# Omega and the first row-wise load on two DMA queues, the activation table first, and more tiles for batch 0's rows

## The chip, the core and the metric

The kernel runs on one core of a Trainium2 chip. A core has a matrix engine (TensorE, PE; its weight loads are shown as PEld), a vector engine (VectorE, DVE), a scalar engine (ScalarE, ACT), a general engine (GpSimd, POOL) and a synchronisation engine (SyncE, SP) that here issues the DMA transfers. Each engine works through its own instruction list in order and waits on semaphores. The metric is the device time of one execution in microseconds (us), lower is better.

## The reference

Three stages follow one another. The first is linear attention with exponential random features, for 4 batches of 8 heads, 576 rows and 64 columns; the other two are feed-forward layers over the 2304 resulting rows of 512.

```python
def phi(x):                                   # x = q*scale or k*scale
    proj = np.einsum('bhsd,md->bhsm', x, omega)          # 128 features
    sq = np.sum(x * x, axis=-1, keepdims=True) / 2.0
    h = proj - sq
    h = h - np.max(h, axis=-1, keepdims=True)
    return np.exp(h) / np.sqrt(m)
q_p, k_p = phi(q_s), phi(k_s)
kv = np.einsum('bhsm,bhsd->bhmd', k_p, v);  z = np.sum(k_p, axis=2)
out = einsum(q_p, kv) / (einsum(q_p, z) + 1e-06)
x = out.transpose(0, 2, 1, 3).reshape(B * S, H * D)      # 2304 x 512
h = np.maximum(x @ w_in, 0.0);  x = h * h @ w_out        # 512 -> 2048 -> 512
xn = x / rms * rms_g;  out = (silu(xn @ w_gate) * (xn @ w_val)) @ w_out2   # 512 -> 1536 -> 512
```

## The kernel before, in words

The kernel is written as a list of steps (`plan.add`): each has an engine, an estimated duration, a priority, a function that emits its instructions, and the buffers that it reads and writes. `Plan.run` (line 113) simulates these steps on the engines with the estimated durations, takes the ready step with the lowest priority number on each free engine, gives out tiles from numbered classes (`slots`, line 301) as they come free, and so writes the order in which the instructions stand on every engine. What the simulation decides is fixed in the program; on the chip each engine follows that order and waits by semaphores where an input isn't there. A step may have alternatives on another engine (`alts`); the planner takes the one that it expects to end first. Three constants matter here: matrix steps count double before `COLD`; from 0.6 to 45.0 us of planned time (`FILL`) the planner puts pairs of dummy matmuls with a matrix of ones (line 480) where TensorE has nothing to do; a DMA (line 383) occupies the SyncE queue for its bytes at 311 KB per us and lands 2.0 us later.

Attention goes batch by batch (`attention(b)`, line 519) and in it by four pairs of heads. A pair loads transposed k and q (tile classes `lt` and `tt`), row-wise k and q (class `ld`, three tiles) and v. The row-wise loads are only for the squared norms: one step squares the tile in place (line 496; on GpSimd, ScalarE or VectorE, lines 498 to 500), a VectorE step sums it (line 531). The feature matmuls (line 577) take the transposed loads and `oms`, which is omega turned and scaled. Maxima are taken on VectorE (line 584), the two corrections join them (line 589), and ScalarE takes the exponentials (line 596). Products with v, transposes and a division follow, and the pair's result is split in two parts of reduced width for the dense stage (lines 392 and 401). What is left of 576 rows after 512 is loaded for all heads at once (`rest_t`, `rest_r`, `rest_v`).

The first feed-forward layer (`moe1`) has for each batch 16 blocks of hidden units: line 804 is its first product, line 834 its second. While batch 0 is in this layer its weights are loaded, decoded on VectorE and ScalarE (lines 430 to 444) and split; attention of batch 1 is interleaved with it. Class `f` has four tiles, which hold the outputs of `relu` in that layer (line 818). The second feed-forward layer comes last (lines 1046 and 1107).

At the start, omega is loaded twice by two transfers on SyncE's queue (line 386, called from line 486), into the lower and the upper 64 partitions of `om2`; ScalarE scales it into `oms` (line 489). That instruction is the first one on ScalarE, and the load of the activation table stands in front of it.

Of the kernel before, what the change touches and what calls it, by code (L numbers as in the profile page):

```python
# [9 lines left out]
F32 = mybir.dt.float32  # L10
# [4 lines left out]
AF = mybir.ActivationFunctionType  # L15
ALU = mybir.AluOpType
# [26 lines left out]
class Plan:  # L43
# [8 lines left out]

    COLD = 6.9
    FILL = (0.6, 45.0, 0.21)
    SPARE = {"DVE": 1.0, "ACT": 0.2, "POOL": 0.2}
    SPARE_TO = 200.0
# [54 lines left out]
    def run(self):  # L113
# [9 lines left out]
        slot = {}  # L123
        engs = sorted({n.eng for n in self.nodes})
        ready = {e: [] for e in engs}
        busy = {e: 0.0 for e in engs}
        held_by = {"DVE": 0.0}
        events = []
        seq = 0
# [1 line left out]
        def push(t, kind, n):  # L131
            nonlocal seq
            seq += 1
            heapq.heappush(events, (t, seq, kind, n))
# [17 lines left out]
        avail = {}  # L152
        for n in self.nodes:
            if n.ndeps == 0:
                push(0.0, 0, n)
        spare_bank = None
        if self.filler:
            c = self.filler[0].classes[0]
# [4 lines left out]
        while done < len(self.nodes):  # L163
# [4 lines left out]
            while events and events[0][0] <= now + 1e-9:  # L168
                _, _, kind, n = heapq.heappop(events)
# [3 lines left out]
                elif kind == 1:  # L173
# [7 lines left out]
                    for o in n.outs:  # L181
                        o.ndeps -= 1
                        t = now + (self.SAME.get(n.eng, 0.0) if o.eng == n.eng and not n.tail else self.LAT)
# [6 lines left out]
            for e in engs:  # L190
# [5 lines left out]
                while ready[e]:  # L196
                    item = heapq.heappop(ready[e])
                    n = item[3]
# [25 lines left out]
                if pick is not None:  # L224
# [3 lines left out]
                    if isinstance(pick.dur, Shared):  # L228
                        start = max(now, busy["POOL"])
                        held_by["DVE"] = start + pick.dur  # L230
                    busy[e] = start + pick.dur * (2.0 if e == "PE" and now < self.COLD else 1.0)
                    push(busy[e] + pick.tail, 1, pick)
# [5 lines left out]
        for n in order:  # L238
            for b in n.acq:
                c, s = slot[b]  # L240
                t = self.alloc[c](s)
# [6 lines left out]
def kernel(  # L248
# [23 lines left out]
    nc = tc.nc  # L272
    PSUM = bass.MemoryType.PSUM
    B, SR, H, _ = rest_v.shape
    _, HP, P, _, R, D = q_r.shape
# [10 lines left out]
    SCALE = float(D) ** -0.25  # L286
# [4 lines left out]
    const = ctx.enter_context(tc.tile_pool(name="const", bufs=1))  # L291
# [16 lines left out]
    plan = Plan(slots)  # L308
# [38 lines left out]
    ones = const.tile([P, P], F32R, name="ones")  # L347
    om2 = const.tile([P, M], F32, name="om2")
    oms = const.tile([P, M], F32, name="oms")
    g_sb = const.tile([P, KC], F32, name="g_sb")  # L350
    eps_sb = const.tile([P, 1], F32, name="eps_sb")
    v_t = [att.tile([P, 2, R, D + 1], F32, name=f"v{i}") for i in range(2)]
    vr_t = att.tile([P, H * (D + 1) + 8], F32, name="vr")[:, :H * (D + 1)].rearrange("p (h n) -> p h n", h=H)
    kv_t = [att.tile([P, 2, 80], F32, name=f"kv{i}")[:, :, :D + 1] for i in range(2)]
# [4 lines left out]
    b_oms = Buf(ap=oms)  # L359
# [7 lines left out]
    def f32(t):  # L367
        return t.bitcast(F32)
# [11 lines left out]
    def pe(n, cnt, passes=1):  # L380
        return cnt * passes * max(0.109, 0.0133 + n / 2400.0)

    def dma(prio, outap, inap, nbytes, r=(), w=(), after=()):
        return plan.add(
            "SP", nbytes / 311e3, prio,
            lambda: nc.sync.dma_start(out=outap(), in_=inap()), r, w, after, tail=2.0,
        )

# [21 lines left out]
    def load_unit(prio, dst, src, r=(), after=()):  # L410

        wap, c = src
        wide = wap.dtype != F32
        words = 2 if wide else 1
        a = wap[c].bitcast(U32) if wide else wap[c]
        o = (lambda: dst.ap.rearrange("p n t -> p (n t)")) if wide else (lambda: dst.ap)
        dma(prio, o, lambda: a, 262144 * words, r=list(r), w=[dst], after=after)
# [43 lines left out]
    T0 = -40.0  # L461
# [10 lines left out]
    b_late, b_eps = Buf(ap=ones), Buf(ap=eps_sb)  # L472
# [8 lines left out]
                             rhs=ones.rearrange("p (o n) -> p o n", o=1).to_broadcast([P, 2, P]), start=True, stop=True)  # L481

    plan.filler = Buf(["acc"]), filler
    b_om = Buf(ap=om2)
    for h in range(2):
        dma(T0, lambda h=h: om2[h * D:(h + 1) * D, :], lambda: omega_t, 32768, w=[(b_om, h)])
    dma(T0 + 30, lambda: g_sb, lambda: rms_g.rearrange("(k p) -> p k", p=P), 2048, w=[b_g])

    plan.add("ACT", 0.4, T0, lambda: nc.scalar.activation(out=oms, in_=om2, func=AF.Copy, scale=SCALE), [b_om], [b_oms])

    def copy(prio, out, src, n, rd, wr):

# [26 lines left out]
    def attention(b):  # L519
# [7 lines left out]
        def row_norms(prio, x, ss):  # L527
            square(prio, x, lambda: x.ap, 512)
            plan.add(
                "DVE", dve(512), prio,  # L530
                lambda: nc.vector.tensor_reduce(out=ss.ap[:, :8], in_=x.ap, op=ALU.add, axis=AX), [x], [ss],
            )

        def operand(ldp, src, cls):

            x = Buf(["lt", cls])
            dma(ldp, lambda: x.ap, src, 262144, w=[x])
            return x

        def rem_prep(pr0):  # L540
            rem_x[:] = [operand(lead, lambda: rest_t[b].rearrange("p h n -> p (h n)"), "tr")]
            xr = Buf(["ld"], view=lambda t: t.rearrange("p h r d -> p (h r) d"))
            dma(lead, lambda: xr.ap, lambda: rest_r[b], 262144, w=[xr])
            row_norms(pr0, xr, ssr)
            dma(lead, lambda: vr_t[P - SR:], lambda: rest_v[b], 133120, w=[b_vr])

        def pair(hp):
# [7 lines left out]
            ld = pb - 3.0  # L555
# [3 lines left out]
            def transposed(nm, p0):  # L559
                ss = stats[nm] = Buf(["sm"])  # L560
                src, src_t = (k_r, k_t) if nm == "k" else (q_r, q_t)
                xs = operand(ld, lambda: src_t[b, hp], "tt")
                x = Buf(["ld"], view=lambda t: t.rearrange("p h r d -> p (h r) d"))
                dma(ld + 0.05, lambda: x.ap, lambda: src[b, hp].rearrange("p h r d -> p (h r) d"), 262144, w=[x])
                row_norms(p0, x, ss)
                return xs

# [35 lines left out]
            u = step / 10.0  # L603
            pk, pq = Buf(["p"]), Buf(["p"])
            xk = transposed("k", pb)
            features(pb + u, pk, xk, ODD, stats["k"], list(last_q))
            if hp == 0:
                rem_prep(pb + u)
                rem_p[:] = [Buf(["pr"])]
                features(pb + 2 * u, rem_p[0], rem_x[0], ODD, ssr)  # L610
            pr = rem_p[0]
            xq = transposed("q", pb + 2 * u)
            last_q[:] = [features(pb + 4 * u, pq, xq, ODD, stats["q"])]

# [558 lines left out]


    attention(0)
    for b in range(B):
        if b + 1 < B:
            attention(b + 1)
        moe1(b)
# [104 lines left out]
```

## Time and profile before

| | us |
|---|---|
| median of three runs | 972.69 (971.24 to 972.92) |
| the profiled execution, its own time | 972.6 |
| its span, first to last instruction | 970.8 |
| TensorE busy in it | 955.1 |
| VectorE busy | 688.4 |
| ScalarE busy | 518.6 |
| GpSimd busy | 78.8 |

The profile is one execution. The times of rows are microseconds from the start of the span unless marked ns. A row of a timeline names start, length, engine, line, operation and tiles (out <- in); in brackets stands how long the engine had been idle before, and what ended that. SPq is the issue of a DMA on SyncE. PE's granted clock is shown as a share of 2.4 GHz. A table by stretch gives for each stretch its length, the busy time of PE, PEld, DVE, ACT and POOL with the number of instructions, the granted clock, the busy share of the DMA engines, and the GB/s that they moved.

### The profile page before, as it was taken

What the parts mean: (1) busy time and instruction counts of PE and PEld (TensorE: products, weight loads), DVE (VectorE), ACT (ScalarE), POOL (GpSimd) and SP (SyncE); (2) the same over time, 40 slices, a digit from 0 to 9 for tenths busy, and PEclk for the clock granted to TensorE, in tenths of its full rate; (3) what the DMA queues carried; (4) which work ended last, traced back from release to release, by engine and by line L of the source; (5) the groups of instructions that cost most, each with busy time, mean ns of one, the idle gap of its engine ahead of it and who ended that gap; (6) DMA issues with size and microseconds to landing.
All of it is one profiled execution on the core that took longest, in us unless ns stands there. A gap on an engine that the chain in (4) does not pass through costs nothing.

```text
span 970.8 us, 16150 instructions
## 1 busy us (share of the span) xinstructions
PE 955.1 (98%) x6036; PEld 793.0 (82%) x6036; DVE 688.4 (71%) x1241; ACT 518.6 (53%) x1078; POOL 78.8 (8%) x69
## 2 busy tenths in 40 slices
PE   8999999999999999999999999999999999999998
PEld 7877777787888788788889888888878888888886
DVE  5889988756747556645745889989897757577573
ACT  6987788656446446445645658554443452323220
POOL 1123312000101010000100110000000000000000
PEclk9999999999999999999999999999999999999999
DMA  7878788888678565598978444324233221222203
GB/s 248 271 255 285 245 283 310 284 305 293 223 238 284 185 222 176 181 309 280 317 254 316 127 142 124 105 88 133 87 107 131 77 76 33 77 61 59 70 29 108
DMA packets 74845, 179.45 MB, mean 185 GB/s; under 512 B 8848, under 2 KB 12048, under 8 KB 74768
## 3 DMA queue, kind: packets, MB, share of 16 engines
q1 hardware_dynamic: 74768, 178.43, 56.0%
q8 instruction: 47, 0.77, 0.3%
q14 instruction: 30, 0.25, 0.1%
HBM read 143.27 MB, written 35.13 MB: 184 GB/s over the span
## 4 chain that ended last, share of the span: by engine, by line
PE 82%; DVE 8%; DMA 4%; ACT 3%; issue 1%; POOL 1%; SPq 0%; POOLq 0%; DVEq 0%; ACTq 0%
PE h L804 17%; PE acc L834 17%; PE acc L1046 12%; PE t L1107 11%; PE h L1046 11%; PE t L1046 4%; PE t L577 3%; DMA st<-in_w_gate_dram 1%; DMA ld<-in_k_r_dram 1%; PE t L692 1%; PE t L635 1%; DVE cc L1066 1%; PE acc L480 1%; PE t L686 1%; PE h L1107 1%
## 5 line engine op out<-in xcount | busy, mean ns | idle before, releaser
L834 PE MATMUL acc<-g,wr 128*128 128x512 f32 (+1 forms) x660 | 151.5, 373 | 1.2 <-POOL g L392 1.2
L804 PE MATMUL h<-x,wr 128*128 128x512 f32 x528 | 134.6, 398 | 0.0
L834 PEld LDWEIGHTS acc<-g,wr 128*128 128x128 f32 x660 | 113.4, 189 | 22.2 <-POOL g L392 1.4
L401 ACT CAST wq<-wq 128x512 fp32r<-128x512 f32 x108 | 66.5, 619 | 103.2 <-DMA wq<-w2d4g 15.8
L1107 PE MATMUL t<-wq,ub 128*128 128x512 f32 x474 | 116.7, 391 | 1.4 <-DVE oa L1115 1.3
L804 PEld LDWEIGHTS h<-x,wr 128*128 128x128 f32 x528 | 97.6, 189 | 21.7
L1046 PE MATMUL acc<-x,wq 128*128 128x512 f32 x324 | 106.9, 389 | 0.0
L1107 PEld LDWEIGHTS t<-wq,ub 128*128 128x128 f32 x474 | 88.4, 188 | 22.2 <-DVE oa L1115 2.9
L392 DVE TENSOR_TENSOR wq<-wq 128x512 fp32r<-128x512 f32 x108 | 79.7, 745 | 30.4 <-ACT wq L401 30.0
L818 ACT ACTIVATE f<-h 128x512 f32<-128x512 f32 (+1 forms) x80 | 44.9, 562 | 90.1 <-PE h L804 90.1
L1046 PE MATMUL h<-x,wq 128*128 128x512 f32 x252 | 85.3, 390 | 0.0
L392 DVE TENSOR_TENSOR g<-f,g 128x512 fp32r<-128x512 f32 (+1 forms) x61 | 39.6, 650 | 45.6 <-ACT f L499 34.5
L1046 PEld LDWEIGHTS acc<-x,wq 128*128 128x128 f32 x324 | 60.8, 188 | 12.8 <-DVE cc L1066 0.2
L1046 PE MATMUL acc<-xa,wq 128*128 128x512 f32 x192 | 69.8, 389 | 0.0
L834 PE MATMUL acc<-g,wu 128*128 128x512 f32 (+1 forms) x300 | 68.3, 373 | 0.0
L1066 DVE TENSOR_TENSOR cc<-acc,cc 128x512 f32<-128x512 f32 x84 | 57.8, 688 | 14.3 <-PE acc L1046 13.1
L1115 DVE TENSOR_TENSOR oa<-t,oa 128x512 f32<-128x512 f32 x75 | 50.9, 688 | 21.8 <-PE t L1107 21.3
L596 ACT ACTIVATE p<-t,sm 128x128 f32<-128x128 f32 x212 | 57.8, 382 | 14.2 <-DVE sm L589 12.2
L439 ACT ACTIVATE dw<-st 128x512 f32<-128x512 f32 x68 | 46.4, 692 | 29.2 <-DMA st<-in_w_out_dram 8.7
L804 PE MATMUL h<-x,wu 128*128 128x512 f32 x240 | 61.5, 399 | 0.0
L1046 PE MATMUL h<-xa,wq 128*128 128x512 f32 x168 | 60.5, 389 | 0.0
L834 PEld LDWEIGHTS acc<-g,wu 128*128 128x128 f32 x300 | 51.7, 189 | 9.6
(213 smaller groups left out, 1641.5 us busy)
## 6 DMA issues: line engine op xcount, KB each, us to landing
wr<-w1d SPq DMA_DIRECT2D x88, 512.0 KB, 4.6
st<-in_w_out_dram SPq DMA_DIRECT2D x28, 512.0 KB, 4.9
w1d<-wr SPq DMA_DIRECT2D x22, 512.0 KB, 4.3
st<-in_w_in_dram SPq DMA_DIRECT2D x16, 512.0 KB, 4.5
st<-in_w_gate_dram SPq DMA_DIRECT2D x12, 512.0 KB, 5.5
st<-in_w_val_dram SPq DMA_DIRECT2D x12, 512.0 KB, 5.2
st<-y SPq DMA_DIRECT2D x23, 256.0 KB, 4.2
v<-in_v_r_dram SPq DMA_DIRECT2D x16, 260.0 KB, 4.2
```

The costliest lines, as they stand in the source:

```text
L392: return lambda: en.tensor_tensor(out=lo(), in0=src(), in1=f32(hi()), op=ALU.subtract)
L401: first = plan.add("ACT", act(n), prio, lambda: nc.scalar.copy(out=hi(), in_=src()), rd, [whi], after, pre=[blo] if blo is not bhi else [])
L439: lambda: nc.scalar.activation(out=out(), in_=hf(), func=AF.Abs, scale=65536.0), [(st, 1)], [w])
L577: nc.tensor.matmul(fps[h].ap[:, i, :], lhsT=x.ap[ps, c], rhs=oms[ps, :], start=True, stop=True)
L596: nc.scalar.activation(out=pbuf.ap[:, j, :], in_=fp.ap[:, i, :], func=AF.Exp, bias=mx.ap[:, j:j + 1])
L804: nc.tensor.matmul(hb.ap[:, :n], lhsT=u.ap[:, wl, kk * P:(kk + 1) * P], rhs=xcols(j, xl, kk)(), start=(gi == 0 and ii == 0), stop=(gi == l ...
L818: lambda: nc.scalar.activation(out=rb.ap[:, :n], in_=hb.ap[:, :n], func=AF.Relu), [hb], [rb])
L834: nc.tensor.matmul(accs[e].ap[:, :n], lhsT=u.ap[:, w, es], rhs=x.ap[:, :n], start=(c == 0 and i == 0), stop=(c == C1 - 1 and i == 2))
L1046: nc.tensor.matmul(bank.ap[:, cols], lhsT=u.ap[:, wl, c0 + kk * P:c0 + (kk + 1) * P], rhs=x[kk][xl].ap[:, :cols.stop - cols.start], start= ...
L1066: lambda: nc.vector.tensor_tensor(out=out.ap, in0=bank.ap, in1=x.ap, op=ALU.add), [bank, x], [out])
L1107: nc.tensor.matmul(o.ap, lhsT=x[xl].ap[:, c0:c0 + P], rhs=us[f"o{i}"].ap[:, wl, :], start=i == n == 0, stop=i == 1 and n == 2)
L1115: lambda: nc.vector.tensor_tensor(out=oa.ap, in0=o.ap, in1=oa.ap, op=ALU.add), [o, oa], [oa])
```

## The change

Omega's second half is loaded by a DMA that ScalarE issues; so is the first row-wise k of batch 0, whose priority is raised to that of omega. An exponential of one column of ones is written to a new small tile (`warm`), so that it is ScalarE's first activation. Omega is scaled on VectorE. The row-wise loads of batch 0 (k, q and the rest) may take a tile of class `f` where no `ld` tile is free. In the planner, all engines begin at 0.75 us, matrix steps count double until 8.0 us, a DMA on SyncE occupies the queue for at least 0.45 us, and one on ScalarE occupies that engine for 0.6 us and lands 2.6 us later.

```diff
--- before.py
+++ after.py
@@ -52,7 +52,8 @@
 
 
 
-    COLD = 6.9
+    BEGIN = 0.75
+    COLD = 8.0
     FILL = (0.6, 45.0, 0.21)
     SPARE = {"DVE": 1.0, "ACT": 0.2, "POOL": 0.2}
     SPARE_TO = 200.0
@@ -123,7 +124,7 @@
         slot = {}
         engs = sorted({n.eng for n in self.nodes})
         ready = {e: [] for e in engs}
-        busy = {e: 0.0 for e in engs}
+        busy = {e: self.BEGIN for e in engs}
         held_by = {"DVE": 0.0}
         events = []
         seq = 0
@@ -152,7 +153,7 @@
         avail = {}
         for n in self.nodes:
             if n.ndeps == 0:
-                push(0.0, 0, n)
+                push(self.BEGIN, 0, n)
         spare_bank = None
         if self.filler:
             c = self.filler[0].classes[0]
@@ -349,6 +350,7 @@
     oms = const.tile([P, M], F32, name="oms")
     g_sb = const.tile([P, KC], F32, name="g_sb")
     eps_sb = const.tile([P, 1], F32, name="eps_sb")
+    warm = const.tile([P, 1], F32, name="warm")
     v_t = [att.tile([P, 2, R, D + 1], F32, name=f"v{i}") for i in range(2)]
     vr_t = att.tile([P, H * (D + 1) + 8], F32, name="vr")[:, :H * (D + 1)].rearrange("p (h n) -> p h n", h=H)
     kv_t = [att.tile([P, 2, 80], F32, name=f"kv{i}")[:, :, :D + 1] for i in range(2)]
@@ -380,9 +382,11 @@
     def pe(n, cnt, passes=1):
         return cnt * passes * max(0.109, 0.0133 + n / 2400.0)
 
-    def dma(prio, outap, inap, nbytes, r=(), w=(), after=()):
+    def dma(prio, outap, inap, nbytes, r=(), w=(), after=(), act_queue=False):
+        if act_queue:
+            return plan.add("ACT", 0.6, prio, lambda: nc.scalar.dma_start(out=outap(), in_=inap()), r, w, after, tail=2.6)
         return plan.add(
-            "SP", nbytes / 311e3, prio,
+            "SP", max(0.45, nbytes / 311e3), prio,
             lambda: nc.sync.dma_start(out=outap(), in_=inap()), r, w, after, tail=2.0,
         )
 
@@ -481,12 +485,15 @@
                              rhs=ones.rearrange("p (o n) -> p o n", o=1).to_broadcast([P, 2, P]), start=True, stop=True)
 
     plan.filler = Buf(["acc"]), filler
-    b_om = Buf(ap=om2)
-    for h in range(2):
-        dma(T0, lambda h=h: om2[h * D:(h + 1) * D, :], lambda: omega_t, 32768, w=[(b_om, h)])
+    b_om, b_warm = Buf(ap=om2), Buf(ap=warm)
+    dma(T0, lambda: om2[:D], lambda: omega_t, 32768, w=[(b_om, 0)])
+    dma(T0, lambda: om2[D:], lambda: omega_t, 32768, w=[(b_om, 1)], act_queue=True)
+    plan.add("ACT", 1.4, T0 + 6.0, lambda: nc.scalar.activation(out=warm, in_=f32(ones[:, :1]), func=AF.Exp), [b_late],
+             [b_warm], after=[plan.nodes[-1]])
     dma(T0 + 30, lambda: g_sb, lambda: rms_g.rearrange("(k p) -> p k", p=P), 2048, w=[b_g])
 
-    plan.add("ACT", 0.4, T0, lambda: nc.scalar.activation(out=oms, in_=om2, func=AF.Copy, scale=SCALE), [b_om], [b_oms])
+    plan.add("DVE", 0.2, T0, lambda: nc.vector.tensor_scalar(out=oms, in0=om2, scalar1=SCALE, scalar2=None, op0=ALU.mult),
+             [b_om], [b_oms])
 
     def copy(prio, out, src, n, rd, wr):
 
@@ -531,6 +538,9 @@
                 lambda: nc.vector.tensor_reduce(out=ss.ap[:, :8], in_=x.ap, op=ALU.add, axis=AX), [x], [ss],
             )
 
+        def by_rows(t):
+            return t.rearrange("p h r d -> p (h r) d") if len(t.shape) > 2 else t.rearrange("p (n d) -> p n d", d=D)
+
         def operand(ldp, src, cls):
 
             x = Buf(["lt", cls])
@@ -539,7 +549,7 @@
 
         def rem_prep(pr0):
             rem_x[:] = [operand(lead, lambda: rest_t[b].rearrange("p h n -> p (h n)"), "tr")]
-            xr = Buf(["ld"], view=lambda t: t.rearrange("p h r d -> p (h r) d"))
+            xr = Buf(["ld"] if b else ["ld", "f"], view=by_rows)
             dma(lead, lambda: xr.ap, lambda: rest_r[b], 262144, w=[xr])
             row_norms(pr0, xr, ssr)
             dma(lead, lambda: vr_t[P - SR:], lambda: rest_v[b], 133120, w=[b_vr])
@@ -560,8 +570,9 @@
                 ss = stats[nm] = Buf(["sm"])
                 src, src_t = (k_r, k_t) if nm == "k" else (q_r, q_t)
                 xs = operand(ld, lambda: src_t[b, hp], "tt")
-                x = Buf(["ld"], view=lambda t: t.rearrange("p h r d -> p (h r) d"))
-                dma(ld + 0.05, lambda: x.ap, lambda: src[b, hp].rearrange("p h r d -> p (h r) d"), 262144, w=[x])
+                x = Buf(["ld"] if b else ["ld", "f"], view=by_rows)
+                dma(T0 if b == hp == 0 and nm == "k" else ld + 0.05, lambda: x.ap,
+                    lambda: src[b, hp].rearrange("p h r d -> p (h r) d"), 262144, w=[x], act_queue=b == hp == 0 and nm == "k")
                 row_norms(p0, x, ss)
                 return xs
 
```

## Rows read from the trace of the kernel before

**Rows 1.** The page's busy times: engine, us, share of the span, instructions

```profile
PE 955.1 (98%) x6036; PEld 793.0 (82%) x6036; DVE 688.4 (71%) x1241; ACT 518.6 (53%) x1078; POOL 78.8 (8%) x69
```

**Rows 2.** Table by stretch: stretches of the prologue and after it

```profile
20.00:54.00 34.00, 32.82 (x504) 28.26 (x503) 30.73 (x85) 30.59 (x86) 5.12 (x4) 1.00 0.84 288
...
60.00:80.00 20.00, 19.78 (x142) 15.69 (x141) 18.22 (x30) 18.32 (x46) 8.77 (x7) 1.00 0.70 226
...
240.00:300.00 60.00, 60.00 (x450) 48.23 (x449) 37.03 (x81) 32.04 (x74) 3.59 (x5) 1.00 0.71 237
```

**Rows 3.** Timeline of the first 12 us, all engines

```profile
0.74 1.22 SPq L386 DMA_DIRECT2D om<-in_omega_t_dram  x2
...
0.83 0.17 DVE L464 MEMSET ones<- 128x128 f32 x1 [0.83 <-PEq L1272]
...
1.05 2.64 PEld L480 LDWEIGHTS acc<-ones 128*128 128x128 f32 x12 [1.05 <-DVE ones L464]
...
2.00 0.58 SPq L386 DMA_DIRECT2D lt<-in_k_t_dram  x1
...
3.10 0.43 SPq L386 DMA_DIRECT2D ld<-in_k_r_dram  x1
...
3.61 1.28 ACT L489 ACT_TABLE_LOAD   x1 [3.61 <-DMA om<-in_omega_t_dram]
...
5.27 1.78 PEld L577 LDWEIGHTS t<-oms,lt 64*128 64x128 f32 x16 [1.58 <-ACT oms L489]
...
7.24 1.27 ACT L499 ACTIVATE ld<-ld 128x512 f32<-128x512 f32 x2 [2.02 <-DMA ld<-in_k_r_dram]
...
7.90 0.69 DVE L531 TENSOR_REDUCE sm<-ld 128x8 f32<-128x512 f32 x1 [6.90 <-ACT ld L499]
...
10.56 0.63 ACT L499 ACTIVATE ld<-ld 128x512 f32<-128x512 f32 x1 [2.05 <-DMA ld<-in_rest_r_dram]
...
11.09 2.15 ACT L596 ACTIVATE p<-t,sm 128x128 f32<-128x128 f32 x8
```

**Rows 4.** Chain that ended last, first 20 us: start, length, what

```profile
4.53 5.25 DMA tr<-in_rest_t_dram
...
14.67 2.59 PE acc L480 x20
```

**Rows 5.** Chain that ended last, 40 to 62 us

```profile
44.90 4.77 DMA ld<-in_k_r_dram
...
54.47 5.91 PE h L804 x18
```

**Rows 6.** Waits from 40 to 54 us: total, times, longest

```profile
ACT ld L499 <- DMA ld<-in_k_r_dram: 1.2, 1, 1.2
```

**Rows 7.** Table by stretch, single microseconds before and in the dense stage

```profile
52.00:53.00 1.00, 0.48 (x2) 0.29 (x2) 0.95 (x3) 0.99 (x3) 0.37 (x1) 1.00 0.74 299
...
55.00:56.00 1.00, 1.00 (x4) 0.81 (x3) 1.00 (x3) 0.67 (x2) 0.00 (x0) 0.50 0.69 234
```

**Rows 8.** Chain that ended last, near 100 us

```profile
100.18 3.00 PE h L804 x12
```

**Rows 9.** Table by stretch, the first transfers

```profile
3.10:4.10 1.00, 0.88 (x5) 0.59 (x3) 0.00 (x0) 0.49 (x1) 0.00 (x0) 1.00 0.82 196
4.10:8.10 4.00, 2.83 (x26) 2.83 (x28) 0.20 (x1) 1.96 (x4) 0.00 (x0) 1.00 1.02 353
```

**Rows 10.** VectorE to 54 us, by line: busy us, mean ns, idle before

```profile
L444 DVE SCALAR_TENSOR_TENSOR dw<-dw,st 128x512 uint32<-128x512 uint32 x4 | 2.7, 685 | 0.0
...
L435 DVE SCALAR_TENSOR_TENSOR st<-st 128x512 uint32<-128x512 uint32 x3 | 2.0, 683 | 0.0
...
L392 DVE TENSOR_TENSOR wr<-dw,wr 128x512 fp32r<-128x512 f32 x2 | 1.3, 671 | 0.0
```

**Rows 11.** Waits of SyncE's queue, 0 to 20 and 20 to 46 us

```profile
SPq L386 <- DVE sm L531: 1.1, 2, 0.8
...
SPq L386 <- DVE sm L531: 2.1, 2, 1.5
```

## The prediction

> **What bounds the kernel now.** I read the page's busy shares first. TensorE is busy for 98% of the span [rows 1], so time can be won in two ways only: less matmul work, or matmul work that starts earlier. The diff touches no matmul, so the second is the question. The table by stretch says where TensorE is full with useful work: from 54 us on it is busy nearly all the time (60.00 of 60.00 us in the third row) [rows 2]. Between 20 and 54 us it looks full as well, but there it runs the dummy matmuls of line 480 in its pauses, and VectorE (30.73 of 34.00 us) and ScalarE (30.59) are the engines that carry the attention of batch 0 [rows 2]. So the first 54 us are a prologue: what ends it earlier moves the whole rest of the kernel forward, and what only fills it does nothing.
>
> The start of the prologue, in order of time [rows 3]: SyncE needs from 0.74 to 1.96 us for the two omega loads, and only then issues the transposed k (2.00) and, fourth in line, the row-wise k (3.10). ScalarE waits for omega until 3.61, loads its table for 1.28 us, and scales omega; the first feature matmul starts at 5.27. The dummy matmuls stand at 0.22 us each (2.64 us for 12), nearly twice what they take later (20 in 2.59 us, [rows 4]). ScalarE's first square waits 2.02 us for the row-wise k, until 7.24, and VectorE does nothing useful before 7.90. ScalarE waits again, 2.05 us, for the rest rows until 10.56; the exponentials of the first pair stand behind that square and start at 11.09. The chain that ended last goes through the transposed rest load (5.25 us from issue to landing), then through TensorE, with 20 dummies of 2.59 us among it [rows 4].
>
> The end of the prologue, again by the chain [rows 5]: a row-wise k of batch 1 is issued at 44.90 and lands 4.77 us later; ScalarE, which works in order, stands 1.2 us before it [rows 6]; then come VectorE's last split and the dense matmuls of line 804 at 54.47. TensorE had been busy for 0.48 of the microsecond from 52 to 53, and from 55 to 56 its granted clock was 0.50, the lower level (1.2 of 2.4 GHz) [rows 7]. Eighteen matmuls took 5.91 us there [rows 5], where 12 of the same shape take 3.00 later [rows 8], so 18 would take 4.5: the lower clock costs 1.4 us.
>
> **The change part by part.**
>
> *Omega on two queues, scale on VectorE, table early.* The second half is issued beside the first instead of after it: half of 1.22 us, 0.61, earlier, so about 3.0 instead of 3.61 [rows 3]. The scaling on ScalarE stood behind the table load, which ended at 4.89; on VectorE nothing stands in front of it. No row has this operation; the nearest are VectorE's 128x128 memset of 0.17 us [rows 3] and its 128x512 passes of 0.68 [rows 10]: 0.2 to 0.7, and I take 0.2 by the like shape. Scaled omega is then ready at 3.2 to 3.7 instead of 5.2. The new wait on VectorE for omega has nothing behind it that could run. The table load (1.28) and the small warm activation lie on ScalarE between about 2 and 4 us, before any square; cover 1.6 us or more before the earliest square that I expect (5.2). Were that cover gone, the 1.3 us would stand before the first square. The trace shows no DMA issued from ScalarE. I take SyncE's 0.6 per omega half, with a bound of twice that above; a gain below it is excluded only in so far as ScalarE has nothing else to do then.
>
> *But the matmul has another wait behind that one.* The transposed k is issued at 1.39 instead of 2.00. It had landed before 5.27; it now shares the DMA engines with the row-wise k, 0.26 MB at 353 GB/s [rows 9], so up to 0.74 us later than its earlier issue would give. And the planner writes dummies until its own estimate of the first feature matmul, which the change puts later (start at 0.75, at least 0.45 per issue, a DMA tail of 2.6 on ScalarE): I estimate 18 to 20 dummies instead of 12, and 20 x 0.22 us from 1.05 on end at 5.45. So the first feature matmul lies between 4.4 and 5.5; I take 5.0, hardly 0.3 us won. On the credit side TensorE has no pause there any more, so it may come to its later, shorter durations sooner; half of the time of 16 feature matmuls (1.78 us) is the bound, 0.9 us [rows 3].
>
> *Row-wise k on ScalarE's queue.* Issued at about 1.4 to 2.0 instead of 3.10, so landing at 5.5 to 6.1 instead of 7.24 if it takes as long; VectorE's first reduction moves from 7.90 to 6.2 to 6.8, at best 2.0 us earlier (5.9). SyncE loses two issues (0.61 and 0.47): the later loads are issued 1.1 us earlier. What the engines move decides whether they land so much earlier. From 3.1 to 4.1 us they moved 196 GB/s, then 353 [rows 9]. Filling that microsecond is worth (353 - 196) x 1.0 / 353 = 0.44 us, and the flow begins 0.61 earlier: 1.05 us. The rest rows land 1.05 us earlier, and with them the exponentials behind their square: 11.09 becomes 10.0. **Start: -1.05 us**, bounds -0.3 (the first feature matmul) and -2.0 (VectorE's first reduction); I take the value in between since ScalarE's order ties the exponentials to the rest rows.
>
> The Trainium skill speaks against this part (DMA: Bandwidth & Descriptors, section "Issuing engines are not separate DMA queues"): DMAs of several engines run on the same 16 DMA engines, so a second issuer saves only the sequencer's time. The row of 196 GB/s agrees in that too little had been issued in this one microsecond; at 353 GB/s the rule leaves nothing. By it the part is worth the issue time alone, at most 1.1 us.
>
> *More tiles for batch 0's row-wise loads.* SyncE's queue stood 1.1 and 2.1 us behind reductions that had to free a row tile [rows 11]; it is in order, so weights, operands and rows of batch 1 stood there too. With the four "f" tiles (first used otherwise by line 818 after 54 us) these waits go, and batch 1's row-wise k should no longer reach ScalarE late. What is late next is the queue's wait for operand tiles and the last pair's own chain. On the end of the prologue this is worth the 1.2 us of [rows 6]; bounds 0 (the queue waits for something else just as long) and -1.2. **-1.15 us.** The lower clock may stay as long as it was: bounds 0 and -1.4.
>
> *The planner's constants.* They cost nothing themselves, but shift every estimate, so the written order of every engine changes. No row prices that; I bound it by the low clock that could go (-1.4) and by one unit of weights that comes ahead of the last pair: its three 128x512 passes on VectorE, 0.683 + 0.685 + 0.671 = 2.04 us [rows 10]. I take 0.
>
> Sum: 972.6 (the profiled execution, span 970.8 and 1.8 around it; the median is 972.69) - 1.05 - 1.15 = **970.4 us**.
>
> **The rivals.**
> 1. *The pause before the dense matmuls closes as well.* Then TensorE keeps its clock: 970.4 - 1.4 = 969.0. For it: the pause is short. Against: the dummies end at a fixed planned time (45 us), while the planned start of the dense part moves back.
> 2. *The start doesn't reach the end.* VectorE and ScalarE are busy for 90% between 20 and 54 us [rows 2], and an order written once can lose a microsecond at each pause; the late wait is only exchanged for another. Then between 971.5 (the start alone) and 972.6.
> 3. *Slower: the last pair of batch 0 gets behind a unit of weights.* All plan times move by over a microsecond, weights and attention compete on VectorE from 30 us on, and one unit ahead of the last pair's steps costs 2.04 us; TensorE then pauses longer just before 54 us and runs as much longer at the lower clock, another 1.4. With the start swallowed: 972.6 + 3.4 = 976.0; with the start kept 975.0. It decides from one whole unit on. Against it: nothing in the diff gives weights a better priority.
> 4. *The second queue only slices the same flow, and the tiles bring nothing.* The transposed k loses by sharing (0.74) what its earlier issue won (0.61), and only omega's issue remains, 0.6 us: 972.0. For it: 353 GB/s as soon as enough is issued [rows 9]. Against: 196 before. This is what the section of the Trainium skill named above would make of the second queue.
>
> **How the numbers follow.** Forecast 0.40 (970.4, own range 969.6 to 971.2; three quarters of it under 970.7), rival 1 0.15, rival 2 0.27, rival 3 0.14, rival 4 0.04. This kernel's measurement can tell some 0.2%, 1.95 us: faster is under 970.7, slower over 974.6. Faster 0.30 + 0.15 = 0.45; same 0.10 + 0.27 + 0.04 = 0.41; slower 0.14. The range leaves out rival 3 above. Below, rival 1 with the start at its far bound (-2.0 instead of -1.05) gives 968.0; above, the swallowed start (972.6) with the first feature matmul at 5.5 and ScalarE's table after all in the way (0.2 + 0.6) gives 973.4. So 968.0 to 973.4.
>
> **What would show it.** Right: scaled omega at 3.2 to 3.7 us; the first square at 5.2 to 6.1; first exponentials near 10.0; the 1.2 us wait of ScalarE near 50 us gone; the dense matmuls of line 804 at about 52.3, still with some microseconds at 0.50. Wrong: exponentials at 11 us or later (start not won); line 804's dense part at 54 us or later in spite of a good start (order binds); granted clock 0.50 for much more or none of it; or new idle time of TensorE after 60 us, which would mean that the decoding of the weights had become the bound.

## The result and the profile after

The changed kernel takes 979.12 us (median, 976.81 to 979.98) beside 971.97 for the kernel before on the same chip: ratio 1.0076, 95% interval 1.0057 to 1.0096. It is slower by 7.2 us, on the other side of the forecast and outside its range. The profiled execution took 979.39 us, with a span of 977.6.

The page of after, busy times by engine, to be read against [rows 1]:

```profile
PE 961.1 (98%) x6032; PEld 789.2 (81%) x6032; DVE 686.8 (70%) x1251; ACT 511.5 (52%) x1070; POOL 78.0 (8%) x68
```

TensorE is busy 6.0 us longer than in [rows 1], with nearly as many instructions (6032 and 6036). The loss is no wait: it is time in which TensorE works. The tables by stretch (columns: stretch, length, busy us and count of PE, PEld, DVE, ACT, POOL, PE's clock, DMA share, GB/s) show the second feed-forward layer, first of before, then of after:

```profile
550.00:960.00 410.00, 408.61 (x1935) 342.13 (x1936) 311.33 (x476) 176.24 (x302) 13.72 (x10) 1.00 0.29 87
```

```profile
550.00:960.00 410.00, 409.56 (x1906) 335.80 (x1906) 307.83 (x470) 175.41 (x302) 13.77 (x10) 1.00 0.29 85
```

The clock is at its upper level, 2.4 GHz (1.00), in both, and TensorE pauses less in after (0.44 us instead of 1.39). Yet in the same 410 us it starts 29 matmuls fewer. So a matmul takes longer on average. The rows by line say which. Columns: line, engine, operation, tiles, count; shortest, median and longest in ns; first and last start; shape. Before:

```profile
L1046 PE MATMUL acc<-x,wq x324: 389/389/405, 552.8 to 932.4; 128*128 128x512 f32 x162
...
L1046 PE MATMUL acc<-xa,wq x192: 387/389/397, 553.0 to 931.0; 128*128 128x512 f32 x192
L1046 PE MATMUL t<-xq,wq x288: 277/283/283, 752.6 to 952.3; 128*128 128x256 f32 x144
...
L1107 PE MATMUL t<-wq,ub x474: 387/389/506, 589.8 to 965.9; 128*128 128x512 f32 x158
```

After, where the same two lines are 1057 and 1118:

```profile
L1057 PE MATMUL acc<-x,wq x324: 392/393/481, 552.6 to 938.7; 128*128 128x512 f32 x162
L1057 PE MATMUL acc<-xa,wq x192: 388/392/402, 552.8 to 937.3; 128*128 128x512 f32 x192
L1057 PE MATMUL t<-xq,wq x288: 274/280/284, 756.2 to 958.7; 128*128 128x256 f32 x144
...
L1118 PE MATMUL t<-wq,ub x474: 387/396/502, 590.2 to 972.6; 128*128 128x512 f32 x158
```

The median of line 1118 is 7 ns above that of line 1107, of the x matmuls 4 ns; the 256-column ones are 3 ns shorter. Matmuls overlap, so what costs time is the distance from one start to the next. The chains give it for twelve in a row (start, us, what), before and then after:

```profile
620.50 2.72 PE t L1107 x12
```

```profile
621.41 2.80 PE t L1118 x12
624.21 2.76 PE acc L1057 x12
```

2.72/12 is 226.7 ns, 2.80/12 is 233.3, 2.76/12 is 230. Averaged over the layer from the starts in the trace, the 1008 matmuls of 512 columns with x, xa or xb go from 226.9 to 231.5 ns, the 648 of the second product from 227.2 to 233.3, the 288 of 256 columns from 119.8 to 116.8. That makes 1008 x 4.6 + 648 x 6.1 - 288 x 3.0 ns = 4.6 + 4.0 - 0.9 = 7.7 us; less the 0.95 us by which the pauses shrank, 6.8. The marks agree: where a step of VectorE or ScalarE is compared with the same one of after, after is 0.1 us *ahead* at 557 us, 1.5 behind at 663, 3.0 at 734, 5.0 at 830 and 6.8 at the end. The loss grows evenly over 400 us, in a layer that the diff doesn't mention. In the first layer the medians are the same (389 ns at lines 804 and 815).

### The profile page after: what moved, and what is told of

Its sections match the earlier page's. It is cut to its first block, busy times and chain, and to the rows that moved or that the text cites. A ratio compares the mean times of both kernels' runs of the same rounds, so it can differ in the third digit from the quotient of the medians.

```text
span 977.6 us, 16133 instructions
## 1 busy us (share of the span) xinstructions
PE 961.1 (98%) x6032; PEld 789.2 (81%) x6032; DVE 686.8 (70%) x1251; ACT 511.5 (52%) x1070; POOL 78.0 (8%) x68
## 4 chain that ended last, share of the span: by engine, by line
PE 91%; DMA 3%; DVE 3%; ACT 2%; issue 1%; SPq 0%; POOL 0%; POOLq 0%; DVEq 0%; ACTq 0%
PE acc L845 19%; PE h L815 19%; PE acc L1057 13%; PE t L1118 13%; PE h L1057 11%; PE t L1057 3%; PE t L588 3%; PE h L1118 2%; PE t L703 1%; PE t L646 1%; PE t L697 1%; PE acc L484 1%; DMA ld<-in_k_r_dram 1%; DMA st<-in_w_gate_dram 1%; ACT p L607 1%
## 5 line engine op out<-in xcount | busy, mean ns | idle before, releaser
L1118 PE MATMUL t<-wq,ub 128*128 128x512 f32 x474 | 119.4, 397 | 0.4 <-DVE oa L1126 0.3
L845 PE MATMUL acc<-g,wu 128*128 128x512 f32 (+1 forms) x300 | 71.2, 382 | 0.6 <-POOL g L396 0.6
```

Source lines behind the costliest of these rows:

```text
L845: nc.tensor.matmul(accs[e].ap[:, :n], lhsT=u.ap[:, w, es], rhs=x.ap[:, :n], start=(c == 0 and i == 0), stop=(c == C1 - 1 and i == 2))
L1118: nc.tensor.matmul(o.ap, lhsT=x[xl].ap[:, c0:c0 + P], rhs=us[f"o{i}"].ap[:, wl, :], start=i == n == 0, stop=i == 1 and n == 2)
```

## The experiments

### Where the second layer's matmuls got slower: the place of the tiles

The diff does one thing to that layer: `warm`, a tile of 4 bytes per partition, takes 32 bytes of the pool `const`, and everything allocated behind it from the left end of SBUF (f, st, x, g, then xb, xq, ub) moves by 32 bytes. The tiles allocated from the right end (in the second layer xa and wq) don't move. Line 295 of the kernel before holds an unused tile of 32 bytes, `edge`, at that right end. In the addresses that the compiler gave, the tiles on the left and those on the right start at the same remainder by 256 in the kernel before (192 and 192), at 224 and 192 after. (The traces hold no addresses: the two remainders of before are read from the compiler, those of every other kernel below follow from them and the size of its edit.) All matmuls of the second layer have wq (right) as one operand, most of them a left tile as the other; in the first layer both operands lie on the left.

**One edit to the kernel before: only the place.** An unused tile of the same size, at the same point, and nothing else.

```diff
     eps_sb = const.tile([P, 1], F32, name="eps_sb")
+    const.tile([P, 1], F32, name="pad")
```

> The kernel before with one unused tile of 4 bytes per partition (32 with its padding) added behind eps_sb; no instruction and no order changes, only the addresses of the tiles on the left side move by 32 bytes, as the new tile of the change moves them. Theory 1 (address): in the second feed-forward layer the 512-column matmuls stand at 231 to 233 us/1000 apart instead of 226.7, and the time is about 978.4 (972.0 + 6.4). Theory 2 (the new order and tile assignment of that layer is what costs): nothing changes, 972.0 within 1.

Measured: 978.68 us, ratio 1.0074 (1.0049 to 1.0099). A tile that no instruction touches costs what the whole change costs. By line in its trace:

```profile
L1108 PE MATMUL t<-wq,ub x474: 392/396/501, 587.3 to 969.4; 128*128 128x512 f32 x158
```

396 ns as in after. Next, which places are good. In the changed kernel, `warm` of 64 bytes; then the edge tile moved by 32 bytes as well; then the kernel before with the edge tile alone moved.

```diff
-    warm = const.tile([P, 1], F32, name="warm")
+    warm = const.tile([P, 16], F32, name="warm")[:, :1]
```

> The changed kernel with its new tile made 64 bytes wide instead of 4, so that all addresses are again multiples of 64; order of all engines as in the changed kernel. Theory 1 (address): the second layer's matmuls are back at 226.7 ns and the time is 979.1 - 6.4 = 972.7, which is the kernel before within 1 us: the new order itself wins nothing. Theory 2 (order): still 979.

Measured: 978.11, ratio 1.0069 (1.0049 to 1.0089). The expectation that a multiple of 64 bytes is enough fell.

```diff
-    edge.tile([P, 8], F32, name="edge")
+    edge.tile([P, 16], F32, name="edge")
```

> The changed kernel with the unused tile at the right end widened from 32 to 64 bytes, so that right-side tiles, too, start 32 bytes beside a multiple of 64, as the left-side ones do. Theory 1a (what counts is that a matmul's two operands start at the same remainder by 64): second layer back at 226.7 ns, about 972.7, though the features, whose omega stays at a multiple of 64, may lose a little. Theory 1b (what counts is a multiple of 64 for each operand alone): still 979 or slower. Theory 2: still 979.

Measured (this edit in the changed kernel): 979.34, ratio 1.0084 (1.0060 to 1.0108). The left tiles had moved up by 32 bytes, this moves the right ones down by 32: the sides are then 64 apart.

> The kernel before with the unused tile at the right end widened from 32 to 64 bytes: the right-side tiles move to a remainder of 32, the left-side ones stay at multiples of 64. Order unchanged. Theory 1a (the two operands differ): about 978.4, and the second layer's matmuls at 231 to 233 ns, as in the changed kernel, from the other side. Theory 1b: slower too where a right-side tile is an operand. Theory 2: 972.0 within 1.

Measured (the same edit in the kernel before): 977.65, ratio 1.0061 (1.0040 to 1.0082). Here no left tile has moved at all, so it isn't the left side's own place that costs. What was left was that the two sides must agree, and by what. Three kernels test that: the changed kernel with `warm` of 256 bytes (left as before), the changed kernel with an edge tile of 256 bytes (the right side goes to 224, where the left one is), and the kernel before with a pad of 128 bytes.

```diff
-    warm = const.tile([P, 1], F32, name="warm")
+    warm = const.tile([P, 64], F32, name="warm")[:, :1]
```

> The changed kernel with its new tile made 256 bytes wide, so that the left-side tiles move by 256 bytes in all and every dense operand again starts at remainder 192 by 256, as in the kernel before (where left and right side agree). The four earlier runs had remainders 224/192, 0/192, 224/160 and 192/160 for left/right and were all slow, so an agreement by 64 is not enough. Theory 3 (left and right operands must have the same remainder by 128 or 256): second layer at 226.7 ns, 978.7 - 6.4 = 972.3 within 1.5. Theory 4 (the kernel before only happens to be fast, any edit loses it): 978 to 979 still.

Measured: 972.24, ratio 1.0011 (0.9992 to 1.0030), beside 971.13 for the kernel before.

```diff
-    edge.tile([P, 8], F32, name="edge")
+    edge.tile([P, 64], F32, name="edge")
```

> The changed kernel as it is, with the unused tile at the right end widened from 32 to 256 bytes, so that right-side tiles have remainder 224 by 256, as the left-side ones have in it. Theory 3 (only agreement counts): second layer at 226.7 ns, 972.3 within 1.5. Theory 3b (the remainder 192 itself counts): about 979. Theory 4: 978 to 979.

Measured: 972.18, ratio 1.0018 (1.0002 to 1.0034).

```diff
+    const.tile([P, 32], F32, name="pad")
```

> The kernel before with an unused tile of 128 bytes behind eps_sb: left side at remainder 64, right side at 192 by 256, both 64 by 128; no instruction changes. Theory 3 with period 128: 971.3 within 1, second layer at 226.7 ns. Theory 3 with period 256: about 977.7, second layer at 231 to 233 ns. Theory 4: 978 to 979.

Measured: 978.64, ratio 1.0075 (1.0055 to 1.0096). The chains of e5, of e6 and of e7, the second product again:

```profile
620.26 2.72 PE t L1118 x12
```

```profile
620.42 2.72 PE t L1118 x12
```

```profile
621.04 2.78 PE t L1108 x12
```

| kernel | left, right (by 256) | twelve matmuls, us | ratio |
|---|---|---|---|
| before | 192, 192 | 2.72 | 1 |
| e5 | 192, 192 | 2.72 | 1.0011 |
| e6 | 224, 224 | 2.72 | 1.0018 |
| after | 224, 192 | 2.80 | 1.0076 |
| e1 | 224, 192 | 2.79 | 1.0074 |
| e2 | 0, 192 | 2.80 | 1.0069 |
| e3 | 224, 160 | 2.80 | 1.0084 |
| e4 | 192, 160 | 2.80 | 1.0061 |
| e7 | 64, 192 | 2.78 | 1.0075 |

Fast where the sides agree, at both values tried (192 and 224); slow where they differ by 32, 64 or 128. So of the change's 7.2 us, 979.12 - 972.24 = 6.9 go with the place of one small tile (by the differences of the ratios 6.3 with e5 and 5.6 with e6), and with that set right nothing is won: e5 takes 1.1 us more than the kernel before (from 0.8 less to 2.9 more by its interval), e6 1.7 more (0.2 to 3.3). What in the chip does this is not shown. It can't be only that one matmul's own two operands disagree: acc<-xa,wq has both on the right side, and it slowed as well, from a median of 389 to 392 ns, and not only among matmuls that mix the sides: where three of these follow one another, the distance of starts goes from 226.6 to 231.3 ns (49 places in each trace).

### What the parts of the change are worth without that

The five experiments below all have their sides agree (192, 192), so what they show is order and time of work.

**The extra tiles off.** e5 with both choices of class back to `ld` alone:

```diff
-                x = Buf(["ld"] if b else ["ld", "f"], view=by_rows)
+                x = Buf(["ld"], view=by_rows)
```

> The changed kernel with the 256-byte tile, and without the additional tiles for batch 0's row-wise loads (they take class ld alone). By the prediction these tiles win 1.15 us, so this would be that much slower than the changed kernel with the 256-byte tile: 973.4. If the start of the kernel doesn't set its end, the two are the same within 1 us.

Measured: 973.23, ratio 1.0020 (1.0006 to 1.0033), against 1.0011 with the tiles. The difference of 1.0 us is the size that the expectation named, but the intervals overlap: in this order of work the tiles' worth can't be told from none.

**Does a shift of the start reach the end?** The kernel before, with three loads of omega into `oms` put ahead of everything on SyncE's queue (`oms` is overwritten before use):

```diff
+        for _ in range(3):
+            nc.sync.dma_start(out=oms[:D], in_=omega_t)
         plan.run()
```

> The kernel before with three more loads of omega into the scaled-omega tile ahead of everything on SyncE's queue; each waits for the one before it, so omega and all later loads are issued some 4.5 to 5 us later. No engine's order changes otherwise, addresses are as before. It asks whether a shift of the start reaches the end. If it does one to one, as the prediction assumed: 971.1 + 4.8 = 975.9, with the later start seen again at the first dense block near 56 us. If the prologue is bound elsewhere: under 973.

Measured: 976.67, ratio 1.0059 (1.0036 to 1.0081). Its timeline (start, length, engine, line, operation, tiles, idle before):

```profile
5.59 1.24 SPq L386 DMA_DIRECT2D om<-in_omega_t_dram  x2
...
10.09 1.79 PEld L577 LDWEIGHTS t<-oms,lt 64*128 64x128 f32 x16 [6.40 <-ACT oms L489]
```

Omega is issued 4.85 us later than in [rows 3], the first feature matmul comes 4.82 later, the kernel ends 5.2 later (3.5 to 7.9 by the interval; 3.3 by the spans of the two profiled executions, 974.1 and 970.8). A late start is paid for the most part: a delay at the start does reach the end. That a gain does as well is not shown by it.

**The start alone.** The kernel before, in its own order, with its own constants and without the extra tiles; only the issuer of omega's second half and of the first row-wise k, the early exponential, and the engine that scales omega are changed (`warm` has 256 bytes):

```diff
-        dma(T0, lambda h=h: om2[h * D:(h + 1) * D, :], lambda: omega_t, 32768, w=[(b_om, h)])
+        dma(T0, lambda h=h: om2[h * D:(h + 1) * D, :], lambda: omega_t, 32768, w=[(b_om, h)],
+            issuer=nc.scalar if h else None)
...
-    plan.add("ACT", 0.4, T0, lambda: nc.scalar.activation(out=oms, in_=om2, func=AF.Copy, scale=SCALE), [b_om], [b_oms])
+    plan.add("ACT", 0.4, T0, lambda: nc.vector.tensor_scalar(out=oms, in0=om2, scalar1=SCALE, scalar2=None, op0=ALU.mult),
+             [b_om], [b_oms])
```

> The kernel before, with its planned order, and only the edits to the start: omega's second half and the first row-wise k issued by ScalarE, the table loaded by a small exponential behind them, omega scaled on VectorE; the new tile is 256 bytes wide, so that the addresses agree. No additional tiles, planner's constants as before. The prediction's first term: 971.1 - 1.05 = 970.1, scaled omega at 3.2 to 3.9, first exponentials at 10.0 instead of 11.1. Rival (the transfers that follow share the same flow, and the rest rows land as late as before): exponentials at 10.8 or later, 971.1 within 0.5.

Measured: 970.28, ratio 0.9989 (0.9977 to 1.0000), by which it takes 1.1 us less than the kernel before: the shortest time of all, and just at the edge of what can be told from none. Its timeline, then its chain and a row of its table by stretch:

```profile
4.44 0.63 ACT L502 ACTIVATE ld<-ld 128x512 f32<-128x512 f32 x1 [0.98 <-DMA ld<-in_k_r_dram]
...
10.56 0.63 ACT L502 ACTIVATE ld<-ld 128x512 f32<-128x512 f32 x1 [2.22 <-DMA ld<-in_rest_r_dram]
...
11.09 1.12 ACT L610 ACTIVATE p<-t,sm 128x128 f32<-128x128 f32 x4
```

```profile
53.95 1.59 PE h L818 x6
...
55.57 3.02 PE h L818 x12
```

```profile
55.00:56.00 1.00, 0.97 (x5) 0.49 (x4) 1.00 (x3) 0.94 (x3) 0.00 (x0) 1.00 0.81 205
```

The chain of e1, which has the order and the start of before:

```profile
53.24 1.59 PE h L805 x6
...
54.85 3.00 PE h L805 x12
```

The first square comes 2.8 us earlier than in [rows 3], but the rest rows' square and the exponentials stand at 10.56 and 11.09, where they stood before. In this execution (span 1.7 us shorter) the dense matmuls start 0.5 us earlier than in [rows 5] and the eighteen take 4.6 us instead of 5.91: its clock was 1.00 from 55 to 56, where [rows 7] show 0.50. So this one profile shows 0.5 us of start and 1.3 of clock, not the forecast's path through the exponentials. And neither need come from the edits: e1, with the start of before, has these matmuls at 53.24, in 4.59 us and at full clock. One execution differs from the next by as much, so where e10's 1.1 us come from is open.

**The constants back.** e5 with the old planner constants:

```diff
-    BEGIN = 0.75
-    COLD = 8.0
+    BEGIN = 0.0
+    COLD = 6.9
...
-            "SP", max(0.45, nbytes / 311e3), prio,
+            "SP", nbytes / 311e3, prio,
```

> The changed kernel with the 256-byte tile and the planner's constants as before (engines begin at 0, matrix steps double until 6.9, no least time of an issue). If the new constants shift the order so that the start's gain is lost: faster than the changed kernel with the 256-byte tile (972.2) by about 1 us, 971.2 or below. If not: 972.2 within 0.7.

Measured: 974.02, ratio 1.0008 (0.9989 to 1.0026): no difference from e5 that can be measured. Its executions fall into two groups, 969.1 to 970.5 (five) and 974.0 to 976.7 (seven). In six of these seven the mean granted clock is 0.992 or 0.993, in the five 0.997 to 0.999: an estimate from these figures, 0.5% of 970 us, is 4.9 us, the size of the gap. The seventh (974.1 at 0.998) and what lowers the clock in some executions are open.

**The start and the tiles in the order of before.** e10 with class `f` allowed for batch 0's row-wise loads:

```diff
-                x = Buf(["ld"], view=lambda t: t.rearrange("p h r d -> p (h r) d"))
+                x = Buf(["ld"] if b else ["ld", "f"], view=by_rows)
```

> The kernel before with the edits to the start (as in the run with these alone: 970.3) and, in addition, the four further tiles for batch 0's row-wise loads; planner's constants as before, the new tile 256 bytes wide. If the tiles win what the prediction gave them: 970.3 - 1.15 = 969.1. If their order shifts cost what the start wins: 971.0 to 972.5. The second layer's matmuls at 226.7 ns in either case.

Measured: 976.03, ratio 1.0059 (1.0040 to 1.0078), beside 970.84 for the kernel before. Against e10 the tiles cost some 6 us here (5.75 by the medians, 6.8 by the ratios, on two chips). Its second layer runs at about 227 ns a matmul of 512 columns, so it isn't the place. Its chain between 50 and 100 us:

```profile
59.53 2.79 PE acc L851 x11
...
76.36 4.71 DMA st<-in_w_in_dram
...
90.41 3.69 DMA st<-in_w_out_dram
```

From 50.3 to 59.5 us the chain runs over the decoding of weights on VectorE and ScalarE, then over relu and squares, and further on twice through a load of weights; the fifth relu output of the first layer comes 3.4 us later than in e10, the next three 1.7 to 2.9 later. In e10 the chain has no load between 64 and 100 us. So allowing `f` changed which step the planner takes when, and the chain then waits on weights. At the end of the profiled executions 3.2 us are left of this (972.3 against 969.1 of span); the profiled one is the shortest of e12, and where the rest of its 6 us goes is open.

## Why the prediction was wrong, point by point

**The step that failed: "The diff touches no matmul".** From it the prediction concluded that only an earlier start of matmul work could change the time, and it counted `warm` as an instruction on ScalarE alone. The diff allocates a tile, and an allocation moves every tile behind it. No term of the sum, no bound and no rival had that. e1, a tile without any instruction, showed 7.2 us of it (ratio 1.0074), and e5 and e6 took it away from the changed kernel in two independent ways. The code held a hint: an unused tile of 32 bytes at the right end (line 295), without purpose unless something depends on the place of the tiles.

The two terms of the sum failed as well, apart from the place: -1.05 and -1.15 were forecast, and e5 and e6, with the place set right, are 1.1 and 1.7 us slower than the kernel before.

**Start, -1.05: about its size in the order of before, lost in the order of the change.** e10 measured 1.1 us less, its interval from 2.2 less to none; that the size fits may be luck, since its profile shows another route. In the change's order nothing of it shows: e8 has the same start and the new order without the tiles, and is slower than the kernel before (ratio 1.0020, 1.0006 to 1.0033, beside 0.9989, 0.9977 to 1.0000, for e10). So the new order costs some 3 us there (by the ratios, on two chips), which is more than rival 2's lost start. e9 speaks of a delay alone. The timeline of after:

```profile
0.74 0.56 ACTq L387 DMA_DIRECT2D om<-in_omega_t_dram  x1
...
1.05 4.34 PEld L484 LDWEIGHTS acc<-ones 128*128 128x128 f32 x20 [1.05 <-DVE ones L468]
...
1.96 1.28 ACT L491 ACT_TABLE_LOAD   x1 [1.96 <-issue]
...
3.86 0.23 DVE L495 TENSOR_SCALAR oms<-om 128x128 f32<-128x128 f32 x1 [2.87 <-DMA om<-in_omega_t_dram]
4.39 0.69 DVE L507 TENSOR_TENSOR ld<-ld 128x512 f32<-128x512 f32 x1 [0.30 <-DMA ld<-in_k_r_dram]
...
5.66 1.00 PEld L588 LDWEIGHTS t<-oms,lt 64*128 64x128 f32 x16 [0.27 <-issue]
...
10.38 0.63 ACT L506 ACTIVATE ld<-ld 128x512 f32<-128x512 f32 x1 [2.13 <-DMA ld<-in_rest_r_dram]
...
10.92 1.38 ACT L607 ACTIVATE p<-t,sm 128x128 f32<-128x128 f32 x5
```

Right: scaling on VectorE takes 0.23 us (0.2 taken), the table load lies beside other work, 20 dummies end at 5.39 (18 to 20 ending at 5.45 forecast), and the sixteen feature matmuls that follow take 1.00 us instead of 1.78. Off: scaled omega starts at 3.86, after the 3.2 to 3.7 forecast for its end, because omega's half on SyncE's queue now lands 3.0 us after its issue (in the other profiles with this start the scaling begins between 3.17 and 3.92); the first square comes at 4.39, earlier than 5.2 to 6.1; the first feature matmul at 5.66, just outside 4.4 to 5.5. And the exponentials, 10.0 forecast, come at 10.92, 0.17 us before those of [rows 3]: the rest rows are issued 0.8 us earlier but land only 0.18 earlier. In e5's execution of the same order they stand at 10.01, so this term varies by 0.9 us from one execution to the next, nearly as much as was forecast for it. Over all profiles the exponentials stand at 11.02 to 11.81 with the old start (before, e1, e4, e7; mean 11.4) and at 10.01 to 11.09 with the new one (nine kernels; mean 10.7). So some 0.7 us of the 1.1 forecast are won at this point.

The Trainium skill (DMA: Bandwidth & Descriptors, section "Issuing engines are not separate DMA queues") gives a second issuer only the time of issuing, 1.1 us at most by the prediction's reading. The 1.1 us of e10 is no more than that.

**More tiles, -1.15: wrong in its mechanism.** The wait that was to go is still there, and only one load of batch 0 took a tile of `f`. After's waits from 40 to 54 us, the load into `f` by tile, and the waits of SyncE's queue behind the reductions, from 0 to 20 and from 20 to 46 us:

```profile
ACT ld L506 <- DMA ld<-in_k_r_dram: 0.9, 1, 0.9
```

```profile
L390 SPq DMA_DIRECT2D f<-in_q_r_dram x1: 423/423/423, 19.4 to 19.4; - x1
```

```profile
SPq L390 <- DVE sm L538: 1.9, 2, 1.2
...
SPq L390 <- DVE sm L538: 0.7, 1, 0.7
```

ScalarE waits 0.9 us instead of 1.2 [rows 6], and SyncE's queue 2.6 us in all instead of 3.2 [rows 11]. Nor was the wait of 1.2 us a fixed price of the order of before. The same wait in e1, e4 and e7, which have that order, its start and no tiles more:

```profile
ACT ld L500 <- DMA ld<-in_k_r_dram: 0.4, 1, 0.4
```

```profile
ACT ld L499 <- DMA ld<-in_k_r_dram: 0.9, 1, 0.9
```

```profile
ACT ld L500 <- DMA ld<-in_k_r_dram: 0.3, 1, 0.3
```

The low clock after it, 1.4 us in the prediction, is in none of the three (1.00 in each microsecond from 54 to 58 us). The term and the bounds beside it were read from one execution. Measured alone the tiles make no difference that can be told in the change's order (e8 against e5) and cost some 6 us in the order of before (e12 against e10). The prediction took away a wait and left the order as it was; but a free tile changes what the planner may start next. Rival 3, weights ahead of attention, comes nearest to e12, though at another place (the stage after 54 us) and for the tiles rather than the constants.

**Constants, 0: held where it was tested.** e11 against e5: 1.0008 and 1.0011, both with the tiles. Without the tiles the new order costs some 3 us (e8 against e10); how much of that is the constants, and how much the other changes of the plan (ScalarE's issues, the priority of the first row-wise k), no run shows.

**The dense matmuls at 52.3 with some low clock: neither.** They start later, at 55.26, and without the low clock. The chain of after, and its table by stretch:

```profile
55.26 4.60 PE h L815 x18
...
103.47 6.77 DMA ld<-in_k_r_dram
```

```profile
53.00:54.00 1.00, 0.00 (x0) 0.00 (x0) 1.00 (x4) 1.00 (x6) 0.00 (x0) 1.00 0.06 25
...
110.00:115.00 5.00, 3.31 (x24) 2.38 (x23) 3.96 (x8) 4.18 (x9) 1.57 (x1) 0.98 0.46 172
115.00:120.00 5.00, 5.00 (x17) 3.94 (x16) 5.00 (x12) 3.08 (x10) 1.40 (x1) 0.68 0.78 277
```

Eighteen take 4.60 us, as rival 1 had it, but not for its reason: the pause is not closed. TensorE is idle for the whole of the microsecond from 53 to 54, and the dense matmuls run at 1.00 all the same; what makes the clock fall after one such pause and not after another is open. It falls later: a row-wise k lands at 110.24, TensorE is idle for 1.69 of the five microseconds from 110, and from 115 to 120 the clock is 0.68 on average. By 557 us after is level with before, so start, tiles and order together had brought about nothing when the second layer began to lose.

## What to carry to other kernels

Price a new tile twice: by the instructions that use it, and by the tiles that it moves; in a kernel bound by TensorE, print the addresses of the matmul operands before and after, and fill up a small tile so that they keep their relation (here: 252 unused bytes for 6 to 7 us). When busy time of the bounding engine grows at a constant number of instructions, compare the duration of one instruction line by line before any wait. And don't price a change of buffers in a planned kernel by the wait that it removes: the same tiles made no difference that could be told in one order and cost about 6 us in another. Nor price a wait of a microsecond from one execution: the same order showed it at 0.3 to 1.2 us in four profiles.

## What was not expected of the hardware

TensorE's matmuls of 512 columns from fp32r tiles come about every 227 ns when the operands of the two ends of SBUF start at the same remainder by 256 bytes (192 or 224), and every 230 to 234 ns when they differ by 32, 64 or 128. Matmuls of 256 columns go the other way at 32 and 64, from 119.8 to between 116.7 and 117.8 ns, and stay at 120.0 when the sides differ by 128 (e7). That is 1 to 3% of a matmul, and some 7 us of a stage of 415; it shows in no wait and no clock. And a transfer of 32 KB that landed within 2.3 us of its issue when SyncE issued both halves (before, e1, e4, e7) landed after 3.0 when ScalarE issued the other half beside it and the first k loads followed at once (2.4 to 3.1 for the later half over the nine profiles with this start); what delays it is not shown.
